# Cosine attention followed by a gated two-layer product: the first product in the 64-row form of TensorE between the score chunks, gated columns freed batch by batch

## The chip, the cores and the metric

One core of a Trainium2 chip. The metric is device time of a whole execution in microseconds. Four to eleven executions of each kernel were timed beside executions of the kernel before on the same chip; nearly all were fast.

## The reference, cut to what matters

```python
# q, k, v: (8 batches, 12 heads, 448 positions, 64), float32
q_n = q / (norm(q) + 1e-6);  k_n = k / (norm(k) + 1e-6)
attn = softmax(q_n @ k_n.T / tau)            # per batch and head
x = (attn @ v).transpose(0, 2, 1, 3).reshape(8 * 448, 768)
h = x @ w_in                                 # 768 -> 2048, "first product"
g = h * sigmoid(1.702 * h)                   # "gate"
out = g @ w_out                              # 2048 -> 768, "second product"
```

## The kernel before

The kernel works on pairs of heads: 6 pairs per batch, 48 in all. A planner inside it (class `Plan`) takes a list of operations with estimated durations, due times and slots, plays them through, and emits the instructions of every engine in the order that comes out. So the order on each engine is fixed when the kernel is built; the chip only waits on semaphores.

The scores of a pair contract over 64, so TensorE runs them in its 64-row form: two matmuls side by side, one on each half of its rows, into two PSUM banks. All else contracts over 112 or 128 rows. One chunk of keys is 112 wide, and a group does two chunks:

```python
def scores(x, c0):
    for c in (c0, c0 + 1):
        sp = sps[x, c] = ps_s.tile([128, 2, 512], FP32, name="sp")
        for j in range(2):                       # the two heads: rows 0-63 and 64-127
            nc.tensor.matmul(out=sp[:, j, :S], lhsT=keys(x, j, c),
                             rhs=queries(x, j, 0, S), start=True, stop=True)

def mm1(b, m):                                   # first product, one block of 128 columns
    ps = mms[b, m] = ps_m.tile([128, 512], FP32, name="mm")
    for kk in range(KT1):                        # KT1 = 6
        nc.tensor.matmul(out=ps[:, :S], lhsT=w_in_sb[:, kk, 128 * m : 128 * (m + 1)],
                         rhs=xTs[b, kk][:, :S], start=(kk == 0), stop=(kk == KT1 - 1))
# ... (cut) tanh on ScalarE and gate on VectorE write gT, one buffer for two batches;
# slot "g" is taken by the first gate of two batches and given back by their last second product
for u in units:
    after = [prev] if prev else []               # the column blocks of a batch follow each other,
    ...                                          # then its second product
```

PSUM has two double banks for scores (`sp`), one bank for attention (`a`) and three for both products (`mm`).

## Time and profile before

| | before |
|---|---|
| median of 4 executions | 436.98 us (436.47 to 437.72) |
| span of the profiled one | 434.7 us |
| TensorE busy | 97% |
| last matmul begins | 430.9 us |

The prediction shows the lines and reads them.

### The profile page before, as it was taken

What the parts mean: (1) busy time and instruction counts of PE and PEld (TensorE: products, weight loads), DVE (VectorE), ACT (ScalarE), POOL (GpSimd) and SP (SyncE); (2) the same over time, 40 slices, a digit from 0 to 9 for tenths busy, and PEclk for the clock granted to TensorE, in tenths of its full rate; (3) what the DMA queues carried; (4) which work ended last, traced back from release to release, by engine and by line L of the source; (5) the groups of instructions that cost most, each with busy time, mean ns of one, the idle gap of its engine ahead of it and who ended that gap; (6) DMA issues with size and microseconds to landing.
All of it is one profiled execution on the core that took longest, in us unless ns stands there. A gap on an engine that the chain in (4) does not pass through costs nothing.

```text
span 434.7 us, 10541 instructions
## 1 busy us (share of the span) xinstructions
PE 423.3 (97%) x4156; PEld 259.0 (60%) x4156; DVE 239.3 (55%) x615; ACT 307.3 (71%) x491; POOL 148.9 (34%) x200
## 2 busy tenths in 40 slices
PE   7889999999999999999999999999999999999996
PEld 7768886654555555565556655565555655565564
DVE  5776986689876476836784338641552115404400
ACT  5979687957998898879986678766776566314421
POOL 0832999257465625342560604233100000000000
PEclk9999999999999999999999999999999999999999
DMA  8999996969989997598966885555112230021022
GB/s 204 220 208 267 203 203 175 246 170 266 199 200 192 257 242 146 153 179 234 207 134 152 173 198 139 126 119 135 35 25 50 50 98 12 14 74 36 2 72 73
DMA packets 98096, 63.99 MB, mean 147 GB/s; under 512 B 56320, under 2 KB 93056, under 8 KB 98048
## 3 DMA queue, kind: packets, MB, share of 16 engines
q1 hardware_dynamic: 92320, 57.03, 56.3%
q0 software_dynamic: 5696, 6.29, 8.9%
q8 instruction: 32, 0.52, 0.5%
q14 instruction: 16, 0.13, 0.1%
q10 hardware_dynamic: 32, 0.01, 0.0%
HBM read 45.61 MB, written 11.01 MB: 130 GB/s over the span
## 4 chain that ended last, share of the span: by engine, by line
PE 87%; POOL 4%; DVE 3%; ACT 3%; issue 1%; DMA 1%; SPq 0%; POOLq 0%; ACTq 0%; DVEq 0%
PE mm L576 35%; PE mm L514 30%; PE avp L415 8%; PE sp L389 8%; POOL n L310 2%; PE mm L468 2%; PE sp L451 2%; POOL qks L327 1%; DMA k<-in_k_dram 1%; ACT et L400 1%; ACT sq L247 1%; PE tps L359 1%; PE mm L544 1%; DVE n L253 1%; POOL w_out L619 1%
## 5 line engine op out<-in xcount | busy, mean ns | idle before, releaser
L400 ACT ACTIVATE et<-sp 112x896 f16<-112x896 f32 x192 | 167.1, 917 | 34.9 <-PE sp L389 28.5
L576 PE MATMUL mm<-w_out,gT 128*128 128x384 f16 (+1 forms) x912 | 156.3, 324 | 0.0
L514 PE MATMUL mm<-xT,w_in 128*128 128x448 f16 x672 | 135.2, 353 | 1.0 <-ACT ost L588 1.0
L576 PEld LDWEIGHTS <-gT 128*128 128x128 f16 x912 | 84.1, 98 | 64.9 <-issue 15.4
L514 PEld LDWEIGHTS <-w_in 128*128 128x128 f16 x672 | 62.4, 98 | 67.3 <-issue 13.9
L531 DVE SCALAR_TENSOR_TENSOR gT<-th,mm 128x448 f16<-128x448 f16 x112 | 68.5, 616 | 59.0 <-ACT th L524 59.0
L524 ACT ACTIVATE th<-mm 128x448 f16<-128x448 f32 x128 | 70.1, 548 | 37.6 <-PE mm L514 32.3
L253 DVE TENSOR_REDUCE n<-sq 112x8 f32<-112x512 f32 x96 | 63.8, 678 | 17.5 <-ACT sq L247 17.3
L343 POOL CAST vt<-v 112x256 f16<-112x256 f32 x92 | 35.1, 402 | 106.6 <-PE avp L415 77.3
L588 ACT ACTIVATE ost<-mm 128x384 f32<-128x384 f32 (+1 forms) x57 | 27.6, 486 | 44.4 <-PE mm L576 42.9
L426 DVE RECIPROCAL rcx<-avp 128x4 f32<-128x4 f32 x72 | 13.0, 181 | 71.5 <-PE avp L415 71.1
L327 POOL TENSOR_TENSOR qks<-k,y 112x512 f16<-112x512 f32 x36 | 37.5, 1042 | 40.9 <-DVE y L294 23.3
L415 PEld LDWEIGHTS <-et 112*128 112x128 f16 x1152 | 44.7, 97 | 11.2
L415 PE MATMUL avp<-vt,et 112*128 112x65 f16 x1152 | 46.7, 193 | 0.0
L389 PE MATMUL sp<-qkT 64*128 64x448 f16 x288 | 39.7, 354 | 0.0
L327 POOL TENSOR_TENSOR qks<-q,y 112x512 f16<-112x512 f32 x36 | 37.5, 1042 | 0.0
L247 ACT ACTIVATE sq<-k 112x512 f32<-112x512 f32 x48 | 30.6, 637 | 5.1 <-DMA k<-in_k_dram 3.3
L429 DVE TENSOR_TENSOR xf<-avp,rcx 128x256 f16<-128x256 f32 x72 | 30.6, 424 | 2.5
L247 ACT ACTIVATE sq<-q 112x512 f32<-112x512 f32 x48 | 30.5, 636 | 0.3 <-DMA q<-in_q_dram 0.2
L310 POOL TENSOR_TENSOR n<-n,root_of 112x16 f32<-112x16 f32 x6 | 17.4, 2900 | 13.2 <-DVE n L253 13.2
L544 PE MATMUL mm<-xT,w_in 128*128 128x224 f16 x192 | 20.5, 259 | 0.1
L359 PE MATMUL tps<-ident 128*128 128x128 f16 x220 | 17.2, 241 | 2.0 <-POOL ident masks.py:199 1.4
(45 smaller groups left out, 227.7 us busy)
## 6 DMA issues: line engine op xcount, KB each, us to landing
k<-in_k_dram SPq DMA_DIRECT2D x48, 224.0 KB, 4.1
q<-in_q_dram SPq DMA_DIRECT2D x48, 224.0 KB, 4.1
v<-in_v_dram SPq DMA_DIRECT2D x48, 224.0 KB, 3.6
w_in<-in_moe_w_in_dram POOLq DMA_DIRECT2D x2, 1536.0 KB, 16.0
w_out<-in_moe_w_out_dram POOLq DMA_DIRECT2D x2, 1536.0 KB, 15.1
out_dram<-ost SPq DMA_DIRECT2D x7, 336.0 KB, 3.1
out_dram<-ost SPq DMA_DIRECT2D x8, 288.0 KB, 2.7
out_dram<-ost SPq DMA_DIRECT2D x8, 240.0 KB, 2.9
```

The costliest lines, as they stand in the source:

```text
L247: return nc.scalar.activation(out=sqs[x, ti], in_=src, func=AF.Square)
L253: nc.vector.tensor_reduce(out=n2s[grp][:, x - grp[0], ti], in_=sqs.pop((x, ti)), axis=AX.X, op=ALU.add,)
L327: return eng.tensor_tensor(out=qkss[x][:, 1 - ti].rearrange("p c j d -> p j c d"), in0=src, in1=rss[x][:, ti, :, :, None].to_broadcast((P, ...
L343: copy(out=vt[:, :, j, :D], in_=src[:, j]) for j in range(2)
L389: nc.tensor.matmul(out=sp[:, j, :S], lhsT=keys(x, j, c), rhs=queries(x, j, 0, S), start=True, stop=True,)
L400: nc.scalar.activation(out=e[:, : 2 * S].rearrange("p (j s) -> p j s", j=2), in_=sps.pop(key)[:P, :, :S], func=AF.Exp, scale=inv_tau, **kw,)
L415: nc.tensor.matmul(out=ps[:, (D + 1) * t : (D + 1) * (t + 1)], lhsT=exps[x, c][:, q0 : q0 + 128], rhs=values(x, c, D * j, D * j + D + 1), ...
L429: nc.vector.tensor_tensor(out=xfs[x][:, :, j], in0=ps[:, :, j : j + D], in1=r[:, :, None].to_broadcast((128, 4, D)), op=ALU.mult,)
L514: nc.tensor.matmul(out=ps[:, :S], lhsT=w_in_sb[:, kk, 128 * m : 128 * (m + 1)], rhs=xTs[b, kk][:, :S], start=(kk == 0), stop=(kk == KT1 - 1),)
L524: nc.scalar.activation(out=ths[key], in_=mms[key][:, :S], func=AF.Tanh, scale=0.851)
L531: nc.vector.scalar_tensor_tensor(out=gts[b // 2][:, m, (b % 2) * S : (b % 2 + 1) * S], in0=ths.pop((b, m)), scalar=1.0, in1=mms.pop((b, m) ...
L576: nc.tensor.matmul(out=mms[b2, t, n][:, : c1 - c0], lhsT=gts[b2][:, kk, 128 * t : 128 * (t + 1)], rhs=w_out_sb[:, kk, c0:c1], start=(kk == 0),
```

## The change

Its intent is to pay for fewer changes of form. For 22 pairs two blocks of the first product of an earlier batch are computed between the score chunks, in the same 64-row form: each matmul takes half of the contraction rows, two run side by side into two banks, and in the second half the banks swap. To allow first products of a batch beside second products of the one before, gated columns are taken and given back batch by batch. Core of the diff, with cuts:

```diff
+    LAG, JOINT = (0, 1, 1, 2, 2, 2, 2, 2), 3
+    with_mm1 = {}
+    for b in range(JOINT, B):
+        for i in range(HP):
+            x = (b + 1) * HP + LAG[b] + i
+            if x < NPAIR:
+                with_mm1[x] = b, 2 * i
 ...
+    def mm1_d(b, m, part):
+        for i in range(2 * (part == 0)):
+            mms[b, m + i] = bank((b, m + i))
+        for kk in range(KT1):
+            for g in range(2):
+                i = g ^ part
+                rows = slice(64 * g, 64 * (g + 1))
+                insts.append(nc.tensor.matmul(
+                    out=mms[b, m + i][:, :S],
+                    lhsT=w_in_sb[rows, kk, 128 * (m + i) : 128 * (m + i + 1)],
+                    rhs=xTs[b, kk][rows, :S],
+                    start=(part == 0 and kk == 0), stop=(part == 1 and kk == KT1 - 1)))
 ...
+            steps = [("s", x, 0), d(0), ("s", x, 1), ("s", x, 2), d(1), ("s", x, 3)]
+            add(("swap", b, m), "ACT", 0.05, s - URGENT - 50, lambda: nc.scalar.nop(), hold=[d(0)])
 ...
+        rows=64, hold=[("swap", b, m)] * step[3])      # d(1) waits for the swap step
 ...
-        | dict(x=2 * HP, mm=3, th=3, g=1, ost=2, port=1)
+        | dict(x=2 * HP, mm=3, run=3, th=3, g0=KT2, g1=KT2, ost=2, port=1)
 ...
-DMA_ENGINES, DMA_PKT_US, DMA_KB_US = 16, 0.033, 0.035
+DMA_ENGINES, DMA_PKT_US, DMA_KB_US, CAST_KB_US = 16, 0.033, 0.035, 0.044
+START_US = 0.6
-    p_sq = pool("p_sq", 2)
+    p_sq = pool("p_sq", 3)
```

The last lines are small repairs of the planner: when the loads start, how long the transfers of the two weight matrices take, how many dummy transposes are wanted, one more buffer for squares. The products of a batch also lose their fixed order among each other and get new due times, and the planner now names their PSUM banks and keeps slots back for steps that need several. These last points are part of "the new order".

More of the change, by code (lines that the diff above doesn't have):

```diff
@@ L24, with packets, cast_packets @@
 LATE_FROM, LATE_US, URGENT = 80.0, 2.0, 12
-DMA_ENGINES, DMA_PKT_US, DMA_KB_US = 16, 0.033, 0.035
-MOE_FROM, MOE_LAG = 8, 9
-WARM_FROM, WARM, KEEP_WARM, FILL_US, FILL_SPARE, FILL_BANK_US = 1.4, 6.2, 50.0, 0.056, 0.3, 1.0
-def packets(n, nbytes, share=1):
+DMA_ENGINES, DMA_PKT_US, DMA_KB_US, CAST_KB_US = 16, 0.033, 0.035, 0.044
+MOE_FROM = 8
+WARM_FROM, WARM, KEEP_WARM, FILL_US, FILL_SPARE, FILL_BANK_US = 1.4, 5.5, 50.0, 0.056, 0.3, 1.0
+def packets(n, nbytes):
     one = DMA_PKT_US + DMA_KB_US * nbytes / 1024
-    return n * one / DMA_ENGINES, share * one
+    return n * one / DMA_ENGINES, one
+def cast_packets(n, nbytes):
+    one = CAST_KB_US * nbytes / 1024
+    return n * one / DMA_ENGINES, 2 * one
 class Plan:
@@ L41, in __init__, with add @@
         self.ops, self.free, self.turns = {}, dict(slots), []
-    def add(self, name, eng, us, due, emit, after=(), takes=(), frees=(), dma=None, rows=128, hold=(), turn=False):
+        self.idle_banks, self.bank = list(range(slots["mm"])), {}
+    def add(self, name, eng, us, due, emit, after=(), takes=(), frees=(), dma=None, rows=128, hold=(), turn=False, banks=()):
         after = list(after) + list(hold)
@@ L46, in add @@
             self.turns.append((due, len(self.turns), name))
-        self.ops[name] = (eng, us, due, emit, after, takes, frees, dma, rows, hold)
+        self.ops[name] = (eng, us, due, emit, after, takes, frees, dma, rows, hold, banks)
     def emit(self, link, fill):
@@ L97, in order @@
             for e in idle:
-                held = []
+                held, kept = [], {}
                 while idle[e] <= now and ready[e]:
                     due, i = heapq.heappop(ready[e])
-                    _, us, _, emit, _, takes, _, dma, rows, _ = ops[i]
-                    if any(self.free[s] < k for s, k in takes):
+                    _, us, _, emit, _, takes, _, dma, rows, *_ = ops[i]
+                    if any(self.free[s] < k or (k and self.free[s] - k < kept.get(s, 0)) for s, k in takes):
                         held.append((due, i))
+                        kept.update((s, k) for s, k in takes if k > 1 and s != "mm")
                         continue
@@ L106, in order @@
                         self.free[s] -= k
+                        if s == "mm" and k:
+                            self.bank.update((b, self.idle_banks.pop(0)) for b in ops[i][10])
                     out.append((now, i, emit))
@@ L144, in order @@
                 for s, k in ops[i][6]:
-                    if own == (s == "port" or s[0] == "turn"):
+                    if own == (s in ("port", "run") or s[0] == "turn"):
                         self.free[s] += k
+                        if s == "mm" and k:
+                            self.idle_banks.extend(self.bank[b] for b in ops[i][10])
                 for u in users[i]:
@@ L207 @@
     p_x = pool("p_x", 2)
-    p_g = pool("p_g", 1)
     p_th = pool("p_th", 3)
@@ L212 @@
     ps_a = psum("ps_a", 1)
-    ps_m = psum("ps_m", 3)
+    ps_m = psum("ps_m", 1)
     tps0 = ps_a.tile([128, 1024], FP16, name="tps", tag="a")
@@ L221 @@
     w_out_sb = wpool.tile([128, KT2, DM], FP16, name="w_out")
+    gT = wpool.tile([128, KT2, 2 * S], FP16, name="gT")
     vts = [const.tile([P, C, 2, D + 1], FP16, name=f"vt{i}") for i in range(NV)]
@@ L383, in queries, with scores @@
         return qkTs[x][64 * j : 64 * (j + 1), 1, s0:s1]
-    def scores(x, c0):
-        for c in (c0, c0 + 1):
+    def scores(x, c0, n=2):
+        for c in range(c0, c0 + n):
             sp = sps[x, c] = ps_s.tile([128, 2, 512], FP32, name="sp")
@@ L461, in attend_h @@
     def attend_h(x, h):
-        ps = avps[x, h] = ps_m.tile([128, 512], FP32, name="mm")
+        ps = avps[x, h] = bank((x, h, "x"))
         for i in range(2):
@@ L506, with bank @@
     xTs, xfs = {}, {}
-    gts, mms, ths, osts = {}, {}, {}, {}
+    def bank(key):
+        i = plan.bank[key]
+        return ps_m.tile([128, 512], FP32, name=f"mm{i}", tag=f"m{i}")
+    mms, ths, osts = {}, {}, {}
     def mm1(b, m):
-        ps = mms[b, m] = ps_m.tile([128, 512], FP32, name="mm")
+        ps = mms[b, m] = bank((b, m))
         for kk in range(KT1):
@@ L520, in mm1 @@
             )
+    def mm1_d(b, m, part):
+        for i in range(2 * (part == 0)):
+            mms[b, m + i] = bank((b, m + i))
+        insts = []
+        for kk in range(KT1):
[6 more added lines that the diff above has]
+                    rhs=xTs[b, kk][rows, :S],
+                    start=(part == 0 and kk == 0),
+                    stop=(part == 1 and kk == KT1 - 1),
+                ))
+        return tuple(insts)
     def tanh(*key):
@@ L528, in gate @@
     def gate(b, m):
-        if b % 2 == 0 and m == 0:
-            gts[b // 2] = p_g.tile([128, KT2, 2 * S], FP16, name="gT")
         nc.vector.scalar_tensor_tensor(
-            out=gts[b // 2][:, m, (b % 2) * S : (b % 2 + 1) * S],
+            out=gT[:, m, (b % 2) * S : (b % 2 + 1) * S],
             in0=ths.pop((b, m)),
@@ L540, in mm1_h @@
     def mm1_h(h, m):
-        ps = mms[h, m, "h"] = ps_m.tile([128, 512], FP32, name="mm")
+        ps = mms[h, m, "h"] = bank((h, m, "h"))
         for i in range(2):
@@ L552, in gate_h @@
     def gate_h(h, m):
-        if h == 0 and m == 0:
-            gts[0] = p_g.tile([128, KT2, 2 * S], FP16, name="gT")
         halves = lambda t: t.rearrange("p (i s) -> p i s", i=2)
         nc.vector.scalar_tensor_tensor(
-            out=gts[0][:, m : m + 2, h * SH : (h + 1) * SH],
+            out=gT[:, m : m + 2, h * SH : (h + 1) * SH],
             in0=halves(ths.pop((h, m, "h"))),
@@ L573, in mm2 @@
         if part == 0:
-            mms[b2, t, n] = ps_m.tile([128, 512], FP32, name="mm")
+            mms[b2, t, n] = bank((b2, t, n))
         for kk in range(4 * part, 4 * part + 4):
@@ L577, in mm2 @@
                 out=mms[b2, t, n][:, : c1 - c0],
-                lhsT=gts[b2][:, kk, 128 * t : 128 * (t + 1)],
+                lhsT=gT[:, kk, 128 * t : 128 * (t + 1)],
                 rhs=w_out_sb[:, kk, c0:c1],
@@ L625 @@
     plan = Plan(
-        dict(q=NQK, k=NQK, v=4, sq=2, qks=6, vt=NV, qkT=7, sp=2, a=1, exp=NE, xs=3, xf=3)
-        | dict(x=2 * HP, mm=3, th=3, g=1, ost=2, port=1)
+        dict(q=NQK, k=NQK, v=4, sq=3, qks=6, vt=NV, qkT=7, sp=2, a=1, exp=NE, xs=3, xf=3)
+        | dict(x=2 * HP, mm=3, run=3, th=3, g0=KT2, g1=KT2, ost=2, port=1)
     )
@@ L691 @@
                 add(("at", x, h), "PE", 0.48, sh + 1, partial(attend_h, x, h), after=es,
-                    takes=[("mm", 1)], frees=[("exp", 2), ("vt", h)])
+                    takes=[("mm", 1), ("run", 1)], frees=[("exp", 2), ("vt", h)], banks=[(x, h, "x")])
                 add(("nx", x, h), "DVE", 0.65, sh + 1 - (0 if first else URGENT), partial(normalise_h, x, h), after=[("at", x, h)],
@@ L695 @@
                 add(("turn", x, h), "PE", 0.15, sh + 1, partial(turn_h, x, h), after=[("nx", x, h)],
-                    frees=[("xs", 1)])
+                    frees=[("xs", 1), ("run", 1)])
                 add(("x", x, h), "ACT" if x in XA and not h else "DVE", 0.35, sh + 1 - (0 if first else URGENT), partial(turned_h, x, h), after=[("turn", x, h)],
-                    takes=[("x", 1 - h)], frees=[("mm", 1)])
+                    takes=[("x", 1 - h)], frees=[("mm", 1)], banks=[(x, h, "x")])
             continue
+        if x in with_mm1:
+            b, m = with_mm1[x]
+            d = lambda part: ("mm1", b, m, part)
+            steps = [("s", x, 0), d(0), ("s", x, 1), ("s", x, 2), d(1), ("s", x, 3)]
+            add(("swap", b, m), "ACT", 0.05, s - URGENT - 50, lambda: nc.scalar.nop(), hold=[d(0)])
+            for i, step in enumerate(steps):
+                after = [steps[i - 1]] if i else [("qkT", x)] + [("x", y) + h for y in range(b * HP, (b + 1) * HP) for h in ([(0,), (1,)] if y < HALF else [()])]
+                if step[0] == "s":
+                    c = step[2]
+                    add(step, "PE", 0.19, s - URGENT * (i > 0), partial(scores, x, c, 1), after=after,
+                        takes=[("sp", 1)] + [("mm", 2), ("run", 2), (f"g{b % 2}", 2)] * (i == 0), frees=[("qkT", int(c == C - 1))], rows=64,
+                        banks=[(b, m), (b, m + 1)] * (i == 0))
+                else:
+                    add(step, "PE", 1.134, s - URGENT, partial(mm1_d, b, m, step[3]), after=after, frees=[("run", 2 * step[3])],
+                        rows=64, hold=[("swap", b, m)] * step[3])
         for c in range(C):
-            if c % 2 == 0:
+            if c % 2 == 0 and x not in with_mm1:
                 add(("s", x, c), "PE", 0.38, s + c // 2, partial(scores, x, c), after=[("qkT", x)],
@@ L704 @@
             add(("exp", x, c), "ACT", 0.82, s + c // 2 + 0.1, partial(exp, x, c),
-                after=[("s", x, c // 2 * 2)], takes=[("exp", 1)], frees=[("sp", 1)])
+                after=[("s", x, c if x in with_mm1 else c // 2 * 2)], takes=[("exp", 1)], frees=[("sp", 1)])
         for j in range(2):
@@ L715, with mm1_op @@
             takes=[("x", 1)], frees=[("xf", 1)], dma=packets(256, 512))
-    moe = []
-    def moe_due(b):
-        return 2 * HP * (b + 1) + MOE_LAG if b else MOE_FROM
-    def product(name, us, emit, after, takes, frees, tail):
-        moe.append((name, us, emit, after, takes, frees, tail))
+    def mm1_op(b, u, due, frees):
+        key = u if b else u + ("h",)
+        half, m = not b, u[1]
+        after = []
+        if half:
+            after += [("x", x, u[0]) for x in range(HP)]
+        else:
+            after += [("x", x) + h for x in range(b * HP, (b + 1) * HP) for h in ([(0,), (1,)] if x < HALF else [()])]
+        if b == 0:
+            after.append(("w_in", m // 8))
+        name = ("mm1",) + key
+        if b and (b, m // 2 * 2) in paired:
+            name = ("mm1", b, m // 2 * 2, 1)
+        else:
+            add(name, "PE", 1.134, due, partial(mm1_h if half else mm1, *u), after=after, takes=[("mm", 1), ("run", 1), (f"g{b % 2}", 1)], frees=[*frees, ("run", 1)],
+                banks=[key])
+        add(("th",) + key, "ACT", 0.46, due - URGENT, partial(tanh, *key), after=[name], takes=[("th", 1)])
+        add(("g",) + key, "DVE", 0.54, due - URGENT, partial(gate_h if half else gate, *u), after=[("th",) + key],
+            frees=[("th", 1), ("mm", 1)], banks=[key])
@@ new lines, in mm2_op @@
+    def mm2_op(b, t, n, due, frees):
+        b2 = b // 2
+        c0, c1 = cuts(b2, t)[n]
+        split = len(cuts(b2, t)) > 2
+        end = n == len(cuts(b2, t)) - 1
+        for part in range(4):
+            if b:
+                after = [("g", b, m) for m in range(4 * part, 4 * part + 4)]
+            else:
+                after = [("g", h, m, "h") for h in range(1 + (t > 0)) for m in range(4 * part, 4 * part + 4, 2)]
+            after.append(("w_out", min(n, 1)))
+            after += [("mm2", b2, t, n, part - 1)] if part else []
+            if end and t in (3, 6):
+                after += [("mm2", b2, u, i, 3) for u in range(t - 3, t) for i in range(2)] + [("mm2", b2, t, i, 3) for i in range(n)]
+            add(("mm2", b2, t, n, part), "PE", 0.652 * (c1 - c0) / NW, due, partial(mm2, b2, t, n, part), after=after,
+                takes=[("mm", int(part == 0)), ("run", int(part == 0))], frees=[*frees, ("run", 1)] if part == 3 else [],
+                banks=[(b2, t, n)])
+        after = [("mm2", b2, t, n, 3)] + ([("ost", b2, t, n - 1)] if n else [])
+        add(("ost", b2, t, n), "ACT", 0.4, due - URGENT, partial(halve, b2, t, n), after=after,
+            takes=[("ost", int(n == 0))], frees=[("mm", 1)], banks=[(b2, t, n)])
+        if end or split:
+            cols = slice(c0, c1) if split else slice(0, DM)
+            segs = list(segments(b2, t))
+            for i, (i0, rows) in enumerate(segs):
+                alone = split and end and i == 0
+                add(("st", b2, t, n, i), "ACT" if alone else "SP", 0.5, due,
+                    partial(store, b2, t, i0, rows, cols, nc.scalar if alone else nc.sync), after=[("ost", b2, t, n)],
+                    frees=[("ost", int(end and i == len(segs) - 1))], dma=packets(rows, 4 * (cols.stop - cols.start)))
@@ L727 @@
+    paired = set(with_mm1.values())
     for b in range(B):
-        b2 = b // 2
+        m0, m1, m2 = [MOE_FROM + 13 * i for i in range(3)] if b == 0 else [2 * HP * (b + i) + 2 * LAG[min(b + i, B) - 1] for i in (1, 2, 3)]
         units = [(h, m) for h in range(2) for m in range(0, KT2, 2)] if b == 0 else [(b, m) for m in range(KT2)]
-        prev = None
+        solo = [u for u in units if not b or (b, u[1] // 2 * 2) not in paired]
         for u in units:
-            key = u if b else u + ("h",)
-            m, half = u[1], not b
-            after = [prev] if prev else []
-            if half and m == 0:
-                after += [("x", x, u[0]) for x in range(HP)]
-            elif m == 0:
-                after += [("x", x) + h for x in range(b * HP, (b + 1) * HP) for h in ([(0,), (1,)] if x < HALF else [()])]
-            if b == 0:
-                after.append(("w_in", m // 8))
-            last = u == units[-1]
-            prev = ("mm1",) + key
-            product(prev, 1.134, partial(mm1_h if half else mm1, *u), after, [("mm", 1)], [("x", HP * last)],
-                [("th", "ACT", 0.46, partial(tanh, *key), [("th", 1)], []),
-                 ("g", "DVE", 0.54, partial(gate_h if half else gate, *u),
-                  [("g", int(b % 2 == 0 and u == units[0]))], [("th", 1), ("mm", 1)])])
@@ L747 @@
-        tiles = (0, 1, 2) if b % 2 == 0 else (3, 4, 5, 6)
-        for t in tiles:
-            for n, (c0, c1) in enumerate(cuts(b2, t)):
-                end = n == len(cuts(b2, t)) - 1
-                for part in range(4):
-                    if b:
-                        after = [("g", b, 4 * part + 3)]
-                    else:
-                        after = [("g", h, 4 * part + 2, "h") for h in range(1 + (t > 0))]
-                    after.append(("w_out", min(n, 1)))
-                    after += [("mm2", b2, t, n, part - 1)] if part else []
-                    last = t == tiles[-1] and end and part == 3
-                    tail = []
-                    if part == 3:
-                        tail = [("ost", "ACT", 0.4, partial(halve, b2, t, n), [("ost", int(n == 0))], [("mm", 1)])]
-                        split = len(cuts(b2, t)) > 2
-                        if end or split:
-                            cols = slice(c0, c1) if split else slice(0, DM)
-                            segs = list(segments(b2, t))
-                            for i, (i0, rows) in enumerate(segs):
-                                alone = split and end and i == 0
-                                tail.append((("st", i), "ACT" if alone else "SP", packets(rows, 4 * (cols.stop - cols.start)),
-                                    partial(store, b2, t, i0, rows, cols, nc.scalar if alone else nc.sync), [],
-                                    [("ost", int(end and i == len(segs) - 1))]))
-                    product(("mm2", b2, t, n, part), 0.652 * (c1 - c0) / NW, partial(mm2, b2, t, n, part), after,
-                        [("mm", int(part == 0))], [("g", int(last and b % 2))], tail)
@@ L774 @@
-    total, done = sum(u[1] for u in moe), 0.0
-    for name, us, emit, after, takes, frees, tail in moe:
-        b, part = divmod(B * done / total, 1)
-        start, end = moe_due(b), moe_due(b + 1)
-        due = start + (end - start) * part
-        done += us
-        add(name, "PE", us, due, emit, after=after, takes=takes, frees=frees)
-        prev = name
-        for kind, eng, n, e, tk, fr in tail:
-            if kind[0] == "st":
-                add(kind + name[1:], eng, 0.5, due, e, after=[prev], frees=fr, dma=n)
-            else:
-                me = (kind,) + name[1:]
-                before = [prev]
-                if kind == "ost":
-                    me = me[:-1]
-                    if me[-1]:
-                        before.append(me[:-1] + (me[-1] - 1,))
-                add(me, eng, n, due - URGENT, e, after=before, takes=tk, frees=fr)
-                prev = me
+            i = solo.index(u) if u in solo else 0
@@ new lines @@
+            last = u == units[-1]
+            mm1_op(b, u, m0 + (m1 - m0) * (i + 0.5) / max(1, len(solo)), [("x", HP * last)])
+        tiles = (0, 1, 2) if b % 2 == 0 else (3, 4, 5, 6)
+        parts = [(t, n) for t in tiles for n in range(len(cuts(b // 2, t)))]
+        for i, (t, n) in enumerate(parts):
+            last = n == len(cuts(b // 2, t)) - 1
+            frees = [("g0", KT2 * (last and t == 3)), ("g1", KT2 * (last and t == 6))]
+            mm2_op(b, t, n, m1 + (m2 - m1) * i / len(parts), frees)
@@ L794 @@
+    add("start", "SP", START_US, -99, lambda: None)
     for i in range(2):
         add(("w_in", i), "POOL", 1.0, i - 2, partial(load_w_in, i), hold=[("load", "q", HP - 1)],
-            dma=packets(768, 4096, 2), **port)
+            dma=cast_packets(768, 4096), **port)
         add(("w_out", i), "POOL", 1.0, 3 + i, partial(load_w_out, i), hold=[("load", "q", HP + 2)],
-            dma=packets(2048, 1536, 2), **port)
+            dma=cast_packets(2048, 1536), **port)
     nc.scalar.preload_act_table_set("natural_log_exp_and_others")
```

## The prediction

> **What bounds the kernel now.** I read, in this order, the busy shares and the forty slices of the page, then the stretches of the run, then the chain of work that ended last in order of time, then the waits.
>
> ```profile
> PE 423.3 (97%) x4156; PEld 259.0 (60%) x4156; DVE 239.3 (55%) x615; ACT 307.3 (71%) x491; POOL 148.9 (34%) x200
> PE   7889999999999999999999999999999999999996
> ...
> PE 87%; POOL 4%; DVE 3%; ACT 3%; issue 1%; DMA 1%; SPq 0%; POOLq 0%; ACTq 0%; DVEq 0%
> ```
>
> TensorE is full from about 30 us to the end and the chain lies on it for 87% of the span. The next table says where that is not so (columns: window, its length, busy time of each engine with instructions, granted clock, DMA share and rate).
>
> ```profile
> 0.00:36.00 36.00, 30.33 (x461) 24.86 (x462) 23.51 (x73) 27.70 (x48) 13.64 (x24) 1.00 0.99 215
> 36.00:66.00 30.00, 28.95 (x398) 25.20 (x397) 25.83 (x54) 23.65 (x41) 24.64 (x17) 1.00 1.16 217
> 66.00:366.00 300.00, 298.88 (x2887) 170.76 (x2884) 172.79 (x459) 235.22 (x363) 110.63 (x160) 1.00 0.68 156
> 366.00:434.70 68.70, 65.17 (x419) 38.15 (x417) 17.17 (x30) 20.75 (x41) 0.00 (x0) 0.99 0.16 44
> ```
>
> In the first 66 us loads, squares, powers and copies set the pace, and many TensorE instructions are only dummy transposes that keep its clock up. From 66 us on it idles 1.1 us in 300. After 366 us there are no scores any more, only the two products, and the last 3.5 us are the final eviction and store.
>
> A busy TensorE is not one at its peak, so the question is what its time is made of. This piece of the chain (start, length, what) is typical of the first product:
>
> ```profile
> 156.67 1.14 PE mm L514 x6
> 157.80 0.48 PE sp L389 x4
> 158.29 2.38 PE mm L514 x12
> 160.66 0.48 PE avp L415 x16
> 161.15 0.48 PE sp L389 x4
> 161.63 1.24 PE mm L514 x6
> 162.87 0.49 PE avp L415 x16
> 163.36 1.14 PE mm L514 x6
> 164.50 0.48 PE sp L389 x4
> ```
>
> Six matmuls of the first product (448 columns, 128 rows) take 1.14 us, 0.19 each. The six right after scores take 1.24, and the twelve after scores 2.38 = 12 x 0.19 + 0.10. A group of four score matmuls, which run two at a time in 64-row form, should take 2 x 0.19 = 0.38 and takes 0.48. So each change between the 128-row and the 64-row form costs about 0.10 us, in each direction; the starts of single matmuls in the trace give 0.096 going to 64 rows and 0.092 coming back, as means over the 167 changes after 66 us: 15.8 us in all. Adding up those starts from 66 us on (365 us) leaves, beside 343 us of streaming and the 15.8 us of changes, under 6 us for everything else, most of it a few ns per matmul. One real wait is in it:
>
> ```profile
> PE mm L514 <- ACT ost L588: 1.0, 1, 1.0
> ```
>
> That is the first product of batch 1, which waits at 97 us for a PSUM bank.
>
> **What the Trainium skill says.** "TensorEngine Tiling (Array Packing)", section Key Properties: changing the tiling mode drains TensorE. The trace agrees and prices it, 0.09 to 0.10 us. The same page, section Gotcha 1: PSUM Pressure: different row tiles write different PSUM banks and must not be in one bank at a time, software has to see to it. That is what the changed kernel's new wait is for; the kernel before never accumulates in 64-row form, so its trace is silent. "TensorE: Matmul & The Clock Gate", Part 3, The mechanism: its list of what overlaps says that a weight load runs beside a matmul only where the row group differs, though its text also names a background weight buffer. Here the trace sides with the buffer: at 164.44 us the weights of the second score pass are loaded 0.01 us after the matmul of the same row group began, and that pass starts 0.20 us after the first. So passes in 64-row form should follow each other at the full rate.
>
> **The change part by part.**
> (1) For the pairs of heads 26 to 47 (22 of 36 full-width pairs) two column blocks of the first product move between the pair's scores: scores of chunk 0, half of the product in 64-row form (six passes of two matmuls, each on half of the contraction, in two banks), chunks 1 and 2, the other half with the banks swapped, chunk 3. 264 full matmuls become 528 half ones in 264 passes: 264 x 0.19 = 50.2 us either way, so streaming neither gains nor loses. What goes is changes of form. In the two instruction orders I count 216 changes before and 188 after: 144 to 112 from the first full-width first product on, 42 to 46 between the first product of batch 0 and there, 30 and 30 in the start. The ideal would be 44 fewer; in 7 of the 22 pairs the order has attention or second product put between the steps, which costs two changes each. 28 x 0.094 = 2.6 us off the path, because TensorE is the bound where they go.
> (2) The second half must wait until ScalarE has seen the first half done (22 semaphore steps in ScalarE's queue, no data). By durations of the trace: a pass lasts 0.35 us from start to end, ScalarE reacts 0.04 us after a TensorE end, TensorE 0.05 us after a ScalarE end (97.40 to 97.45 at the wait above). From the start of the first half's last pass: 0.35 + 0.04 + 0.02 + 0.05 = 0.46 us. TensorE arrives there after that pass and two score passes, 3 x 0.19 = 0.57 us. It fits with 0.1 us to spare, if ScalarE is free; in its order nothing stands between the exponential of chunk 0 and this step, in all 22 pairs. The exponential itself (0.92 us) of chunk 0 must be out before chunk 2: 0.36 + 0.04 + 0.92 + 0.05 = 1.37 us against 0.19 + 6 x 0.19 + 0.19 = 1.52; that of chunk 1 before chunk 3 has the same 0.15. I put 0.02 us for each half, for weights that can no longer be loaded ahead of a wait: 44 x 0.02 = +0.9 us.
> (3) Gated columns are held batch by batch instead of two batches at once, so first products of one batch lie beside second products of the one before. TensorE was full without it, so it buys freedom of order, worth at most the 1.0 us wait at 97 us; in the new order second products already stand near that place. I put -0.7.
> (4) Small repairs of the planner (start of loads, weight loads' duration, one more buffer for squares) reorder the first 66 us. The order there is nearly the same; dummy transposes rise from 220 to 238, 16 of them before the first real one, where TensorE idles 0.5 us anyway. I put -0.3 with 1.5 either way.
> Sum: -2.6 + 0.9 - 0.7 - 0.3 = -2.7, so 437.4 - 2.7 = 434.7 us.
>
> **The rivals.**
> First, the new wait takes the place of the changes. The 0.1 us of (2) is thin, and ScalarE is 78% busy in the long stretch (235 of 300 us). If a halving or a square before chunk 0's exponential runs late, the swap and chunks 2 and 3 are late with it: 0.15 to 0.3 us in 22 pairs is 3.3 to 6.6 us, and the time would be 437 to 440. For it: one queue in order, and thin margins. Against: in the kernel before the same planner's order left under 2 us of waits in 365 us, so its figures for ScalarE hold.
> Second, PSUM. Two of three banks of the products are held from chunk 0 until both gates are through, about 3.0 us of steps, then two tanh and the last gate: some 5 us. One bank is left for second products, and a group there needs 0.35 + 0.04 + 0.49 + 0.05 = 0.9 us after its last matmul starts before the next may begin. Attention and the next first product are placed into those holes; if they are late, 0.3 us a pair makes 441.
> Third, accumulating side by side in two banks is slower than the scores' single passes. 5 ns a pass would be 1.3 us; no overlap at all would be 50 us. Scores show two banks written at once at full rate, so this gets 2%.
> Fourth, the start. TensorE does about 35 us of real work in the first 66, so a start better aligned could give several us, or lose them; the order gives no reason for more than 1.5.
>
> **Range and chances.** The gain is bounded: all changes after 66 us together are 15.8 us and 28 of 216 go. Waits of the first two rivals push up by 0 to 4 us, the start by 1.5 either way, and runs spread 1.2 us. I take 432.0 to 438.0. Faster by over 2% means below 428.7, 6 us more than the sum, only through the start: 0.05. Slower by over 2% means above 446.2: 0.03. Within 2%: 0.92.
>
> **What would show it.** Right: in the timeline of the changed kernel, twelve half-row matmuls between scores with no bubble at either border, and a part of some 1.14 to 1.17 us; the first product's 128-row group down to 408; waits of TensorE for the ScalarE step near zero; the stretch from 66 us to the last matmul shorter by 2.5 to 3.5 us. Wrong: TensorE waiting for the swap step or for exponentials by tenths of a us in most pairs; half-row parts of 1.3 us or more; more idle time on TensorE in the long stretch than 1.1 us in 300; or first products that start more than 2 us earlier or later than the 95.3 us of before.

## The result, and the profile after

| | before | after |
|---|---|---|
| median | 436.98 us | 433.62 us (433.48 to 433.92) |
| span of the profiled execution | 434.7 us | 431.9 us |
| last matmul begins | 430.9 us | 428.0 us |
| changes of form, in the whole order | 216 | 188 |
| of these after 66 us, and what they cost | 167, 15.8 us | 138, 13.1 us |

The ratio is 0.9923 (0.9904 to 0.9941). Ratios are the mean time of one kernel's fast runs over that of the other's in the same rounds, so not quite the ratio of the medians. The gain is 3.4 us, clear of noise, and within 2%.

Not all of it can be read from the traces. The kernel before spreads more: over the later rounds its executions with a mean clock of 0.999 or more took 435.9 to 437.9 us, those of the changed kernel 433.3 to 433.9. The profiled execution of the kernel before (436.5 us) is one of its faster ones, so the two traces differ by 2.8 us only. What makes the other executions longer no trace shows.

The stretches of the changed kernel (window, length, busy time of each engine with instructions, clock, DMA):

```profile
0.00:36.00 36.00, 31.47 (x499) 26.22 (x500) 23.48 (x74) 28.40 (x50) 13.54 (x24) 1.00 0.97 210
36.00:66.00 30.00, 27.96 (x353) 23.96 (x351) 25.44 (x53) 24.10 (x41) 23.86 (x14) 1.00 1.16 220
66.00:366.00 300.00, 299.55 (x3210) 173.04 (x3209) 176.22 (x470) 234.45 (x367) 111.57 (x163) 1.00 0.68 154
366.00:431.90 65.90, 62.27 (x387) 36.67 (x383) 12.32 (x21) 18.09 (x36) 0.00 (x0) 1.00 0.20 55
```

TensorE is busy for 299.55 of the 300 us instead of 298.88, and the stretch after 366 us is 2.8 us shorter (65.9 against 68.7). TensorE was full before and is full after; the same work fits into less time. How, the chain of the changed kernel shows on one joint pair (start, length, what; each piece reaches to the start of the next):

```profile
318.02 0.29 PE sp L404 x2
318.31 1.14 PE mm L551 x12
319.45 0.38 PE sp L404 x4
319.83 1.14 PE mm L551 x12
320.96 0.19 PE sp L404 x2
321.15 0.59 PE avp L430 x16
321.74 2.60 PE mm L610 x16
324.34 1.14 PE mm L533 x6
325.48 0.48 PE avp L430 x16
```

Line 551 is the half-row first product. Twelve of its matmuls take 1.14 us, just what six full ones take (line 533). The two score chunks in the middle take 0.38 = 2 x 0.19, the plain streaming time, where such a group took 0.48 before. The change into the form is in the 0.29 at 318.02 (0.19 + 0.10), the change out of it in the 0.59 of attention (0.48 elsewhere): one of each for the pair where the kernel before paid two of each. The one long wait of TensorE after 66 us, 1.0 us for a PSUM bank at 97 us, is gone from the list of waits.

Small waits for PSUM banks do remain. They hardly show as idle time, because the matmul before is still running out. The chain shows one of them:

```profile
211.26 0.44 ACT th L562
211.71 0.02 issue
211.73 0.63 DVE gT L567
212.36 0.04 issue
212.40 1.30 PE mm L533 x6
```

A first product waits here until the gate of the joint pair before it gives a bank back. By the starts of the matmuls this costs 0.31 us, the same again at 253 us, and 0.31 us is also what is left of the wait at 97 us (now at 95 us).

The step on ScalarE for which the second half waits can be asked for by its line. After the heading "who waited for it" no engine is listed:

```profile
L746 ACTq EVENT_SEMAPHORE  x22: 17/17/17, 189.1 to 355.5; - x22
its engine sat idle before it (us, times) until:
who waited for it (us, times):
```

### The profile page after: what moved, and what is told of

It is laid out like the page before. It is cut to its first block, busy times and chain, and to the rows that moved or that the text cites. A ratio compares the mean times of both kernels' runs of the same rounds, so it can differ in the third digit from the quotient of the medians.

```text
span 431.9 us, 11064 instructions
## 1 busy us (share of the span) xinstructions
PE 421.3 (98%) x4438; PEld 259.9 (60%) x4438; DVE 237.5 (55%) x615; ACT 305.0 (71%) x491; POOL 149.0 (34%) x200
## 4 chain that ended last, share of the span: by engine, by line
PE 87%; POOL 4%; ACT 4%; DVE 2%; issue 2%; POOLq 0%; ACTq 0%
PE mm L610 34%; PE mm L533 18%; PE mm L551 11%; PE avp L430 8%; PE sp L404 7%; PE tps L374 3%; POOL n L325 3%; PE mm L483 2%; PE sp L466 2%; ACT et L415 2%; POOL qks L342 1%; PE tps L366 1%; ACT th L562 1%; POOL w_out L653 1%; PE mm L506 1%
## 5 line engine op out<-in xcount | busy, mean ns | idle before, releaser
L415 ACT ACTIVATE et<-sp 112x896 f16<-112x896 f32 x192 | 169.9, 922 | 23.9 <-PE sp L404 17.7
L610 PE MATMUL mm<-w_out,gT 128*128 128x384 f16 (+1 forms) x912 | 158.9, 323 | 0.0
L567 DVE SCALAR_TENSOR_TENSOR gT<-th,mm 128x448 f16<-128x448 f16 x112 | 67.1, 616 | 70.6 <-ACT th L562 70.6
L562 ACT ACTIVATE th<-mm 128x448 f16<-128x448 f32 x128 | 67.7, 550 | 32.2 <-PE mm L533 26.9
L533 PE MATMUL mm<-xT,w_in 128*128 128x448 f16 x408 | 85.7, 353 | 0.5
L533 PEld LDWEIGHTS <-w_in 128*128 128x128 f16 x408 | 37.6, 98 | 37.2 <-issue 6.6
L551 PE MATMUL mm<-xT,w_in 64*128 64x448 f16 x528 | 57.1, 349 | 0.0
L430 PEld LDWEIGHTS <-et 112*128 112x128 f16 x1152 | 43.5, 97 | 13.6 <-issue 3.4
L404 PE MATMUL sp<-qkT 64*128 64x448 f16 x288 | 43.8, 353 | 0.0
L551 PEld LDWEIGHTS <-w_in 64*128 64x128 f16 x528 | 25.6, 94 | 21.2 <-issue 0.3
```

Of the source, the lines that this page charges most:

```text
L404: nc.tensor.matmul(out=sp[:, j, :S], lhsT=keys(x, j, c), rhs=queries(x, j, 0, S), start=True, stop=True,)
L415: nc.scalar.activation(out=e[:, : 2 * S].rearrange("p (j s) -> p j s", j=2), in_=sps.pop(key)[:P, :, :S], func=AF.Exp, scale=inv_tau, **kw,)
L430: nc.tensor.matmul(out=ps[:, (D + 1) * t : (D + 1) * (t + 1)], lhsT=exps[x, c][:, q0 : q0 + 128], rhs=values(x, c, D * j, D * j + D + 1), ...
L551: insts.append(nc.tensor.matmul(out=mms[b, m + i][:, :S], lhsT=w_in_sb[rows, kk, 128 * (m + i) : 128 * (m + i + 1)], rhs=xTs[b, kk][rows, :S],
L562: nc.scalar.activation(out=ths[key], in_=mms[key][:, :S], func=AF.Tanh, scale=0.851)
L567: nc.vector.scalar_tensor_tensor(out=gT[:, m, (b % 2) * S : (b % 2 + 1) * S], in0=ths.pop((b, m)), scalar=1.0, in1=mms.pop((b, m))[:, :S], ...
```

## The experiments

Theory: the gain is the number of changes of form that went, at some 0.094 us each, because TensorE is the bound where they went. Rivals: the order, the gating and the planner's repairs carry it; the new wait on ScalarE eats a part; the count does not matter once something else binds.

| kernel | changes of form | median, us | ratio to before (95%) |
|---|---|---|---|
| changed kernel | 188 | 433.62 | 0.9923 (0.9904 to 0.9941) |
| changed kernel again | 188 | 433.57 | 0.9924 (0.9902 to 0.9946) |
| product between scores in the 128-row form | 272 | 442.28 | 1.0128 (1.011 to 1.0146) |
| no joint pairs | 220 | 436.2 | 0.9985 (0.9971 to 1.0) |
| planner's repairs alone | 218 | 435.71 | 0.9967 (0.9947 to 0.9988) |
| no swap of banks (wrong result) | 188 | 433.85 | 0.9936 (0.992 to 0.9952) |
| swap by a real instruction | 188 | 442.63 | 1.0136 (1.0116 to 1.0156) |
| joint pairs from batch 1 on | 188 | 444.71 | 1.0168 (1.0144 to 1.0192) |
| the same, planner stays in a form | 154 | 452.16 | 1.0344 (1.0308 to 1.038) |
| no joint pairs, planner stays in a form | 208 | 436.94 | 0.9988 (0.9965 to 1.0011) |
| other due times | 172 | 431.98 | 0.9885 (0.9859 to 0.991) |

**1. The same places, the other form.** The product between the scores, each half one whole column block in the 128-row form:

```diff
-                i = g ^ part
-                rows = slice(64 * g, 64 * (g + 1))
-                insts.append(nc.tensor.matmul(out=mms[b, m + i][:, :S],
-                    lhsT=w_in_sb[rows, kk, 128 * (m + i) : 128 * (m + i + 1)], rhs=xTs[b, kk][rows, :S], ...
+            insts.append(nc.tensor.matmul(out=mms[b, m + part][:, :S],
+                lhsT=w_in_sb[:, kk, 128 * (m + part) : 128 * (m + part + 1)], rhs=xTs[b, kk][:, :S], ...
```

> The changed kernel with the same places in the order, but the product between the scores done in the 128-row form, one column block per half. TensorE then changes form 272 times instead of 188. Theory (the gain is the changes of form that went): 84 more at 0.094 us are 7.9 us, so about 441.5 us, ratio to before about 1.010. Rival (the gain comes from the order, the gating batch by batch and the planner's repairs, and the form hardly matters): about 434 us, ratio 0.993.

Measured: 442.28 us, 8.7 us above the changed kernel, or 0.10 us for each of the 84 more changes. By the starts of the matmuls, 8.5 us of the difference of the two traces are changes of form. The rival's 434 us is out. A piece of its chain, where a joint pair's steps stand together:

```profile
195.60 0.29 PE sp L404 x2
195.90 1.24 PE mm L548 x6
197.14 0.48 PE sp L404 x4
197.62 1.24 PE mm L548 x6
198.87 0.29 PE sp L404 x2
199.16 0.59 PE avp L430 x16
```

Against the changed kernel's pair, 1.14 became 1.24 twice, 0.38 became 0.48 and 0.19 became 0.29: a tenth at every border that is new. Order, slots and planner are the same in both kernels, so the form alone did this.

**2. No joint pairs.** The switch `JOINT` at 8 instead of 3, so no pair qualifies; gating, order and repairs stay.

```diff
-    LAG, JOINT = (0, 1, 1, 2, 2, 2, 2, 2), 3
+    LAG, JOINT = (0, 1, 1, 2, 2, 2, 2, 2), 8
```

> The changed kernel with no product between scores at all (the joint pairs switched off), so only gating batch by batch, the new order and the planner's repairs are left; 220 changes of form, four more than before. Theory: +0.4 us for the changes, -1.0 us if the wait at 97 us is gone, start the same: 436 to 437 us, ratio 0.998 to 1.001. Rival (order and repairs carry the gain): 434 us, ratio 0.993.

Measured: 436.2 us, ratio 0.9985, as the theory said. From here to the changed kernel it is 2.6 us for 32 changes fewer, 0.08 us each. The joint pairs carry about three quarters of the 3.4 us. The two traces say why it is not 32 x 0.096 = 3.1 us: from 66 us on the changes cost 2.9 us less, and the small waits between passes of 128 rows, those at 212 and 253 us among them, cost 0.7 us more.

**3. The repairs alone,** put into the kernel before (a few constants and one buffer, as in the last lines of the diff above).

> The kernel before with the planner's small repairs alone: start of the loads, duration of the weight loads, dummy transposes, one more buffer for squares. 218 changes of form against 216. Theory (the start gives nothing): 436 to 438 us, ratio 0.998 to 1.002. Rival (a better aligned start gives 1 us or more): ratio below 0.997.

Measured: ratio 0.9967 (0.9947 to 0.9988), 1.4 us faster. Here the theory's "the start gives nothing" fell. Two things are in it: the 1.0 us wait at 97 us is gone in this kernel too, so its going needs neither the new gating nor the new order; and summing the streaming time of all real matmuls begun by 66 us (starts and sizes from the trace) gives 36.3 us of work, against 35.6 in the kernel before. The kernel without joint pairs, which has these repairs and more, has done 35.5 us by then and is 0.8 us slower by the ratios. So the new order seems to give some of the repairs' gain back; as the two intervals overlap, this is likely and not shown.

**4. No swap, no wait.** The second half keeps the banks of the first, so that no bank is written from both row groups and the wait has no reason; the result is wrong.

```diff
-                i = g ^ part
+                i = g
 ...
-            add(("swap", b, m), "ACT", 0.05, s - URGENT - 50, lambda: nc.scalar.nop(), hold=[d(0)])
+            add(("swap", b, m), "ACT", 0.05, s - URGENT - 50, lambda: nc.scalar.nop(), after=[d(0)])
 ...
-                        rows=64, hold=[("swap", b, m)] * step[3])
+                        rows=64)
+                    if step[3]:                # only the planner's order keeps the step
+                        plan.ops[step][4].append(("swap", b, m))
```

> The changed kernel with the same order, but the second half of each joint product keeps the banks of the first (a wrong result on purpose), so no bank is written from both row groups and the wait for ScalarE is not needed and not there. Theory (the wait fits into the 0.1 us that is spare): within 0.5 us of the changed kernel, 433 to 434 us. Rival (the wait costs 0.02 us per half or more, as the prediction put it): 0.9 us or more faster, below 432.8 us.

Measured: 433.85 us, the changed kernel within noise; its order of matmuls is the same and its trace has no such step. The wait costs nothing, and the 0.02 us for each half that the prediction charged is not there.

**5. A slower swap.** The empty step becomes a ScalarE instruction on 448 columns that TensorE waits for.

```diff
-            add(("swap", b, m), "ACT", 0.05, s - URGENT - 50, lambda: nc.scalar.nop(), hold=[d(0)])
+            add(("swap", b, m), "ACT", 0.05, s - URGENT - 50, partial(slow, b, m), hold=[d(0)])
+    def slow(b, m):
+        return nc.scalar.activation(out=junk, in_=w_in_sb[:, 0, :S], func=AF.Copy)
```

> The changed kernel with the semaphore step on ScalarE replaced by a real ScalarE instruction of 448 columns, about 0.5 us, which TensorE has to wait for. Theory (the margin is about 0.1 us): the wait is then 0.35 + 0.04 + 0.5 + 0.05 = 0.94 us against 0.57 us of TensorE work in the 15 pairs where nothing else stands between, so 15 x 0.37 = 5.6 us, more if ScalarE falls behind: 438 to 443 us. Rival (there is far more room, the planner has the halves far apart or TensorE finds other work): under 435 us.

Measured: 442.63 us, 9.0 us slower, so the margin is as thin as reckoned. The list of waits and the place of the joint pair of above:

```profile
PE mm L552 <- ACT junk L562: 5.5, 16, 0.4
```

```profile
318.64 0.58 ACT L562 ACTIVATE junk<-w_in 128x448 f16<-128x448 f16 x1 [0.28 <-PE mm L552]
...
319.27 1.31 PE L552 MATMUL mm<-xT,w_in 64*128 64x448 f16 x12 [0.35 <-ACT junk L562]
```

Sixteen pairs wait, 0.35 us each as idle time. The true price of one is higher, 0.51 us from start to start: TensorE counts as busy while its last matmul runs out (0.35 us long, 0.19 us of it streaming), and that tail is normally covered by the next one. 16 x 0.51 = 8.1 of the 9.0 us; the traces differ by 8.4 us, and two of the four executions, at a clock of 0.996, lift the median. The theory's 5.6 was too small for this and because the instruction took 0.58 instead of 0.5 us.

**6. Joint pairs from batch 1 on** (`JOINT` at 1: 34 pairs).

> The changed kernel with the joint pairs from batch 1 on instead of batch 3 (34 pairs instead of 22). The order still has 188 changes of form, for more pairs get other work put between their steps. Theory (only the count of changes counts): the same as the changed kernel, 433 to 434.5 us. Rival (each joint pair saves by itself): 12 more pairs at 2 changes of 0.094 us are 2.3 us, 431.3 us.

Measured: 444.71 us, 11 us slower than the changed kernel with the same count of changes. Both the theory and its rival missed. TensorE is no longer the bound throughout. Between 110 and 180 us the kernel before and this one have:

```profile
110.00:180.00 70.00, 70.00 (x706) 38.70 (x705) 49.31 (x135) 63.57 (x101) 32.56 (x47) 1.00 0.94 204
```

```profile
110.00:180.00 70.00, 64.61 (x751) 36.11 (x748) 49.83 (x137) 59.00 (x95) 31.20 (x43) 1.00 0.88 184
```

The first number after the length is TensorE: 70.00 of 70 us before, 64.61 here. New waits head its list, products waiting for gates and scores for exponentials:

```profile
PE mm L610 <- DVE gT L567: 2.7, 4, 1.1
PE mm L551 <- DVE gT L567: 1.6, 4, 0.6
PE sp L404 <- ACT et L415: 1.5, 3, 0.9
PE sp L466 <- DVE qkT L378: 1.5, 2, 0.8
PE mm L533 <- DVE gT L567: 1.5, 2, 1.3
```

From 109.5 to 117.3 us the chain runs over squares, reductions, tanh and exponentials and not over TensorE at all. A reading that fits: while ScalarE works off squares and exponentials of the early batches, TensorE was kept full by first products that could run at any time; tied to the scores of a pair, they no longer fill holes. Which slot binds first was not separated.

**7. and 8. A planner that stays in the form it is in.** TensorE's next operation is chosen by due time plus a fine for another form, once with joint pairs from batch 1 on (fine 3), once without joint pairs (fine 4).

```diff
-                    due, i = heapq.heappop(ready[e])
+                    if e == "PE":              # FINE stands for the 3 or 4
+                        ready[e].sort(key=lambda r: (r[0] + FINE * (ops[r[1]][8] != mode), r[1]))
+                        due, i = ready[e].pop(0)
+                        heapq.heapify(ready[e])
 ... (cut) the other engines as before
```

> Joint pairs from batch 1 on, and a planner that stays in the form TensorE is in when something of that form is ready and not much later due. 154 changes of form, 34 fewer than the changed kernel. Theory: 34 x 0.094 = 3.2 us, so about 430.4 us, ratio to before 0.985, if no wait takes their place. Rival (staying in one form delays exponentials and attention and TensorE then waits): no faster than 433.6 us.

> The same planner rule without any joint pairs: 208 changes of form, 8 fewer than the kernel before, all products in the 128-row form. Theory: 8 x 0.094 = 0.8 us and the wait at 97 us gone: 435 to 436.5 us. Rival (the order alone can give what the joint pairs gave): 434 us or less.

Measured: 452.16 us, where TensorE waits most for attention's banks (4.3 us in four waits for VectorE); and 436.94 us in the fast runs of the second, whose profiled run (clock 0.946) is not read. The first has the lowest count of all and is the slowest: a low count is worth its price only while TensorE is full. The second shows that an order without joint pairs, in this form of the rule, doesn't come near the changed kernel.

**9. Other due times.** Only when the products of a batch are due, and by how many pairs they lag, chosen so that fewer joint pairs get other work between their steps.

```diff
-MOE_FROM = 8
+MOE_FROM = 4
-    LAG, JOINT = (0, 1, 1, 2, 2, 2, 2, 2), 3
+    LAG, JOINT = (0, 1, 2, 2, 1, 1, 1, 1), 3
-        m0, m1, m2 = [MOE_FROM + 13 * i for i in range(3)] if b == 0 else [2 * HP * (b + i) + 2 * LAG[min(b + i, B) - 1] for i in (1, 2, 3)]
+        m0, m1, m2 = [MOE_FROM + 13 * i for i in range(2)] + [MOE_FROM + 13 + 17] if b == 0 else [2 * HP * (b + i) + 2 * LAG[min(b + i, B) - 1] + o for i, o in ((1, -1), (2, -1), (3, -2))]
```

> The changed kernel with other due times alone (when the products of a batch are due, and how many pairs after its attention), chosen so that fewer pairs have other work put between their steps: 172 changes of form instead of 188, the same 22 joint pairs. Theory: 16 x 0.094 = 1.5 us less than the changed kernel, about 432 us, ratio 0.989. Rival (the count no longer matters once waits or the start bind): the same as the changed kernel within 0.5 us.

> The changed kernel once more, to have it in the same rounds as the next one. All theories: 433 to 434.5 us, ratio 0.991 to 0.995.

Measured in the same rounds: 431.98 us against 433.57 us of the changed kernel, 1.6 us for 16 changes, 0.10 each. It is the fastest kernel. The intervals of the two ratios overlap a little, so by them the difference is likely rather than settled; but the executions at a clock of 0.998 or more do not overlap (four at 431.3 to 432.3 us, five of the changed kernel at 433.3 to 433.7). Its size is the one forecast. Its profiled run was one of its slower ones (span 432.0 us, clock 0.995, and 0.95 in the first 36 us), so its gain cannot be read from that span. Where the changes went its trace does tell: only 6 of the 16 come from joint pairs left whole (19 instead of 16), the other 10 from the scores of the first two batches, which more often stand together.

## Why the prediction was right

It said 434.7 us in 432.0 to 438.0, and 433.62 us came. It started from 437.4 us, the median of three executions before; with the fourth it is 436.98, so the gain forecast is 2.7 us, and 3.4 came by the medians, 2.8 by the two traces. The bound and the mechanism held; single terms were off, and that the sum fits the traces so well is partly luck.

- *Changes of form, -2.6 us.* Right. After 66 us 29 of them and 2.7 us went. Adding 84 cost 8.7 us, removing the joint pairs cost 2.6 us for 32, removing 16 more gave 1.6 us. One count in it was wrong: it speaks of 7 pairs with other work put between, but 44 - 2 x 7 is not the 32 that it counted. The trace has 6 such pairs and 16 whole ones, 44 - 12 = 32, and sixteen pairs waited in experiment 5.
- *Streaming unchanged.* Right: a half took 1.14 us, the lower end of what the prediction asked for. Summed over all starts, the 264 side-by-side passes take 0.189 us each, as the full matmuls do.
- *The swap, +0.9 us.* The failing term. Its mechanism was right, 0.46 us needed in 0.57 us: nobody waits in the trace. The 0.02 us per half for weights that cannot be loaded ahead is not there, as the run without the wait shows. In the traces 0.7 us of small waits between passes of 128 rows, the second rival's bank waits among them, stand in its place, so this error is nearly cancelled there. The 0.6 us by which the medians exceed the traces is the spread of the kernel before and stays open.
- *Gating batch by batch, -0.7, and repairs, -0.3.* The sum was about right: with the four more changes that its order has (+0.4) it asks for 0.6 us, and the kernel without joint pairs is 0.9 us faster than the one before by the medians, 0.7 by the ratio, 0.6 by the traces. The split was not: the repairs alone gave 1.4 us, with the wait at 97 us among it, and gating with the new order gave nothing and perhaps took 0.8 us.
- *Rivals.* The swap is as near as was feared: a step of 0.58 us on ScalarE in its place cost 9.0 us. PSUM showed a little: a first product waits for a bank behind a joint pair twice, 0.31 us each, and not in every pair as was feared. Slower accumulation did not show. The first two bit in earnest only further out: with 34 pairs, waits for gates and exponentials cost more than any change of form.
- *Signs.* The full first product went down to 408 matmuls, and TensorE's idle time in the long stretch fell to 0.45 us, as asked. One sign of "wrong" did appear: the first product of batch 1 begins at 92.9 us, 2.2 us earlier than before (95.1). It is the order that moved and not the pace: by 95 us TensorE had begun 60.9 us of real work, against 61.4 before, so this sign was badly chosen. "Shorter by 2.5 to 3.5 us from 66 us to the last matmul" held: 361.9 us against 364.8.

## What to carry to other kernels

Where TensorE is full, split its time by the starts of neighbouring matmuls and not by busy share: here 97% busy hid 15.8 us of form changes, and in the changed kernel waits of 0.31 us. A product that contracts over 768 was done here in the 64-row form at no cost in streaming, so it could be put where that form already was; the wait for the swap of banks was free with two score passes in between, while a step of 0.58 us in its place cost 9.0 us. Tying free work to bound work was only good while the bound engine stayed full: more joint pairs made the kernel 11 us slower, and fewer changes of form on top of that made it slower still. Look at the single executions too: part of a gain by medians can be the spread of the kernel before.

## What the Trainium skill lacked or had wrong

- "TensorEngine Tiling (Array Packing)", Key Properties, says that a change of tiling mode drains TensorE and gives no price. Here it is 0.096 us on the way into the 64-row form and 0.093 to 0.096 us on the way back (by what is taken as the time of the score pass before it), and each of 84 added changes cost 0.10 us of the total.
- The same page, When to Use Tiling, speaks of row tiling for contractions of 64 or less. No page says that a contraction of 768 can be split into halves of rows for free: 264 passes of two half-row matmuls took 0.189 us each, as 448-column matmuls on 128 rows do.
- "TensorE: Matmul & The Clock Gate", Part 3, The mechanism, lists that weight loads overlap matmuls only where the row group differs. Six passes in a row on the same two row groups took 1.14 us, no longer than six full matmuls, so loading weights of the same row group cost nothing; the background weight buffer, which its text names, is what fits.
- "TensorEngine Tiling (Array Packing)", Gotcha 1: PSUM Pressure, asks software to keep row tiles out of the same bank and gives no cost. With two passes between, it was nil (433.85 us without, 433.62 with). What happens where the rule is broken no run here shows.
